# The first layers of the last eight chunks: two chunks at a time as seven block products instead of eight, with the combined weights and attention's output passed through memory

## The chip, the cores and the metric

The kernel runs on one core of one Trainium2 chip. TensorE (PE) multiplies matrices into PSUM, VectorE (DVE) and ScalarE (ACT) do the elementwise work, GpSimd (POOL) does almost nothing before the change, and SyncE (SP) issues the transfers between SBUF and memory; its queue is worked off in the order in which it is written. The metric is the time of one execution on the device in microseconds; lower is better.

## What is computed

```python
def phi(x):                                   # x: 8 batches, 8 heads, 576 tokens, 64
    proj = x @ w_phi                          # 128 features
    proj = proj - max(abs(proj), axis=-1)
    return concat([exp(proj), exp(-proj)])    # 256 features
q_p, k_p = phi(q), phi(k)
kv = einsum('bhsf,bhsd->bhfd', k_p, v); z = k_p.sum(tokens)
attn = (q_p @ kv) / (q_p @ z + 1e-6)
x = attn as 4608 tokens x 512
g, val = x @ w_gate, x @ w_val                # 512 x 1536 each
out = (g * sigmoid(g) * val) @ w_out          # 1536 x 512
```

The weights arrive as 64-bit floats and are turned into two 32-bit parts on the chip.

## The kernel before

**Attention.** There are 32 units, one for each batch and pair of heads, called attention 0 to 31 here (`attention(i, rank)`). Units 0 to 7 run "early", with plain fp32 matmuls. Units 8 to 31 are "split": operands are cut into a high and a low part (fp32r), and a product takes three matmuls. In one split unit the steps follow each other: the projections of k (`work<-wbd_hi,ks`) and q (`work<-qs,wst_hi`, `wst_lo`: eight matmuls) on PE; copies to `qx` on ACT (L534); on DVE a transpose (L539), the largest value (L547), six small steps, a transpose back (L559), and a subtraction (L562); on ACT two exponentials (L564, L566) and casts to the high part (L579); on DVE the low part (L582); on PE the numerators, 24 matmuls that begin with `work<-qh,kvh`; on ACT the copies to `num` and `den` (L607, L609); on DVE the division (L616 to L620). Most of these buffers exist once for the split units, so unit i+1 can write `qe` only after unit i has divided. At the end `num` is cut into `xh` and `xl` (L632, L634), the operands of the feed-forward part. There are three sets of `xh` and `xl`.

**Feed-forward.** The 4608 tokens are 12 chunks of 384. A chunk has 12 slices f of 128 features. `first(c, f)` makes the gate and the value of a slice: 2 x 4 x 3 = 24 matmuls of 128x384 into two PSUM banks (`gv<-xh,w_hi`, `gv<-xl,w_hi`, `gv<-xh,w_lo`), then tanh on ACT (L716) and two products on DVE (L718, L721). `parts` cuts the result into `hh` (ACT, L741) and `hl` (DVE, L742), and `second(c, f)` multiplies it by w_out: 9 matmuls of 128x512 into three banks `o`. The high parts of all weights stay in SBUF; the low parts are loaded for each slice (`w_lo<-wlo_dram`, 512 KB for the first layer, 256 KB for the second). Chunks 0 to 2 are "early": their first layers run while the weights are prepared, and chunks 1 and 2 keep the result in memory (`keep`, `fetch`) until their second layers run. After that come chunks 3 to 11, each slice's first layer followed by the second layer of the slice before (`put_off`).

**What sets the order.** Every step is given to `Plan.add` with an engine, a cost, what it depends on, and a rank. `Plan.run` plays the steps through once, on the host, and writes each engine's instructions in the order in which it started them. On the chip each engine then runs its list in that order and waits for whatever comes first in it. On PE, attention has a lower rank than feed-forward, so it goes first when it is ready; on ACT and DVE feed-forward goes first (`FIRST`).

Of the kernel before, what the change touches and what calls it, by code (L numbers as in the profile page):

```python
# [17 lines left out]
P = 128  # L18
# [28 lines left out]

# [11 lines left out]
class Plan:  # L59
# [3 lines left out]
    LAG = {"PE": 220, "ACT": 90, "DVE": 90, "SP": 2000}  # L63
# [24 lines left out]
    def run(self):  # L88
# [11 lines left out]
        def start(e):  # L100
# [33 lines left out]
            for t in s.then:  # L134
                n += 1
                heapq.heappush(events, (freed if t.eng == e and e in ("ACT", "DVE", "PE") else done, n, "dep", t))
# [29 lines left out]
def dve(n):  # L166
    return 150 + 1.04 * n
# [5 lines left out]

def act(n):
    return 190 + 0.86 * n


def pe(n):
    return max(58, 7 + 0.441 * n)
# [7 lines left out]
def favor_attention_moe(ctx: ExitStack, tc: tile.TileContext, qT, kT, v, w_phi, wg, wv, wo, out):  # L187
# [7 lines left out]
    h_dram = tc.dram_tile([EARLY, NFT, P, CH], F32, name="h_dram")  # L195

# [139 lines left out]
    x_ready = {}  # L336
# [4 lines left out]
    def attention(i, rank):  # L341
# [245 lines left out]
        for h in range(2):  # L587
            for part in range(2):
# [4 lines left out]
                def numerators(key=key, h=h, c=c):  # L593
# [12 lines left out]
                free = last.get(("num", i - 1))  # L606
                copied.append(add("ACT", act(SH), lambda key=key, ra=ra, c=c: nc.scalar.copy(  # L607
                    num[ra, c], work[plan.bank[key]][ra, :SH]), [nu, free], rank))
                copied.append(add("ACT", act(SH), lambda key=key, ra=ra, rb=rb, c=c: nc.scalar.activation(  # L609
                    den[ra, c], work[plan.bank[key]][rb, :SH], AF.Copy, bias=1e-6), [nu, free], rank, give=key))  # L610
# [17 lines left out]
            [(base, 0, 0, CH), (base + 1, 0, CH, CH // 2)]  # L628
        for c, at, start, width in cuts:
            src = num[:, start:start + width]  # L630
# [8 lines left out]
        last["num", i] = lo  # L639
# [86 lines left out]
    def keep(c, f, j, made):  # L726

        th_free[j] = h_kept[c, f] = add("SP", P * CH * 4, lambda: nc.sync.dma_start(h_dram[c, f], th[j]), [made], FIRST)

    def fetch(c, f):  # L730
        j = ffn["th"] % TH_SETS
        ffn["th"] += 1
        return j, add("SP", P * CH * 4, lambda: nc.sync.dma_start(th[j], h_dram[c, f]), [h_kept[c, f], th_free[j]], FIRST)
# [13 lines left out]
    def second(c, f, hidden, low):  # L747
        b, ready = hidden
        readers, lo, lo_ready = low
        for t in range(NT):  # L750
            sl = slice(t * P, (t + 1) * P)

            def go(t=t, sl=sl):
                if t == 0:
# [4 lines left out]
                    ((hh[b][:, sl], w2_hi[f]), (hh[b][:, sl], lo), (hl[b][:, sl], w2_hi[f])))])  # L759
# [3 lines left out]
            if f == NFT - 1:  # L763
                if n_out[0] == NCH * NT - 1:

                    halves = [pool.tile([P, DM // 2], F32, name=f"osb_last{k}", tag=tag) for k, tag in enumerate(("num", "den"))]
                    for k, eng in enumerate(("ACT", "DVE")):
                        cols = slice(k * DM // 2, (k + 1) * DM // 2)
                        rows = out[c * CH + t * P:c * CH + (t + 1) * P, cols]

                        def copy(k=k, cols=cols, t=t, o=halves[k]):
                            if k:
                                nc.vector.tensor_scalar(out=o, in0=ps_o[t][:, cols], scalar1=0.5, scalar2=None, op0=ALU.mult)
                            else:
                                nc.scalar.activation(o, ps_o[t][:, cols], AF.Copy, scale=0.5)

                        cp = add(eng, act(DM // 2), copy, [done], FIRST)
                        q = nc.sync if k else nc.scalar
                        add("SP" if k else "ACT", P * DM * 2 if k else 60, lambda q=q, rows=rows, o=halves[k]: q.dma_start(rows, o), [cp], FIRST)
                    continue  # L780
                o = osb[n_out[0] % len(osb)]
                cp = add("ACT", act(DM), lambda t=t, o=o: nc.scalar.activation(o, ps_o[t], AF.Copy, scale=0.5),  # L782
                         [done, out_done.get(n_out[0] - len(osb))], FIRST)
                stored[t] = cp
                out_done[n_out[0]] = add("SP", P * DM * 4, lambda t=t, o=o: nc.sync.dma_start(
# [105 lines left out]
```

## Time and profile before

| | |
|---|---|
| median of 3 runs | 1269.33 us (1268.94 to 1270.84) |
| span of the profiled execution | 1273.1 us, 3.8 us above the median |
| busy share PE, DVE, ACT, POOL | 99%, 69%, 51%, 0% |
| moved by the DMA queues | 168.15 MB, 132 GB/s over the span |
| matmuls of 128x384 into `gv` | 3456 |

A busy PE says little here, since matmuls overlap: one of 128x384 is listed with 337 ns, yet the next one starts some 175 ns after it. Time on PE is therefore read from the chain that ended last, which lists runs of matmuls with start and length. "att i" stands in the text for attention unit i.

### The profile page before, as it was taken

How to read it: one execution, taken by the hardware profiler on the slowest of the kernel's cores; microseconds unless marked ns; L12 is line 12 of the kernel's file. 1: busy time of each engine (PE TensorE's matmuls, PEld its weight loads, DVE VectorE, ACT ScalarE, POOL GpSimd, SP SyncE). 2: the span in 40 equal slices, each digit the busy share in tenths (PEclk: the TensorE clock that was granted, in tenths of full speed). 3: DMA queues.
4: the chain of work that ended last, by engine and by line, in shares of the span. 5: the costliest groups of instructions: out<-in, count | busy, mean ns of one | idle time of the engine just before them, and what ended most of it. 6: DMA issues, size and time to landing. Idle time of an engine off the chain costs nothing.

```text
span 1273.1 us, 19796 instructions
## 1 busy us (share of the span) xinstructions
PE 1262.2 (99%) x7427; PEld 1189.9 (93%) x7427; DVE 876.4 (69%) x1674; ACT 651.5 (51%) x1383; POOL 1.3 (0%) x13
## 2 busy tenths in 40 slices
PE   9999999999999999999999999999999999999998
PEld 8887999999889999999999999999999999999998
DVE  6998999998887778762788888822488886222222
ACT  5787433336676666632765666611466665121211
POOL 0000000000000000000000000000000000000000
PEclk8999999999999999999999999999999999999999
DMA  4543455555564344444433444354444342444443
GB/s 120 144 119 102 140 174 175 174 165 167 159 204 123 112 117 113 148 123 127 129 104 113 129 124 120 105 161 129 125 120 119 105 132 84 124 149 125 149 126 106
DMA packets 112111, 168.15 MB, mean 132 GB/s; under 512 B 52752, under 2 KB 59408, under 8 KB 112016
## 3 DMA queue, kind: packets, MB, share of 16 engines
q1 hardware_dynamic: 111552, 166.64, 44.1%
q8 instruction: 58, 0.95, 0.3%
q14 instruction: 37, 0.30, 0.1%
q10 hardware_dynamic: 464, 0.26, 0.1%
HBM read 143.26 MB, written 23.59 MB: 131 GB/s over the span
## 4 chain that ended last, share of the span: by engine, by line
PE 92%; DVE 4%; DMA 1%; ACT 1%; SPq 1%; issue 0%; DVEq 0%; ACTq 0%
PE gv L282 46%; PE o L282 25%; PE work L282 12%; PE kv L435 8%; PE kv L428 1%; DMA out_dram<-osb 0%; PE o L502 0%; DVE km L410 0%; DVE kp L415 0%; DMA shared<-in_wg_dram 0%; DMA shared<-in_wo_dram 0%; DVE qy L491 0%; DMA wbd<-in_w_phi_dram 0%; DVE km L486 0%; ACT den L609 0%
## 5 line engine op out<-in xcount | busy, mean ns | idle before, releaser
L282 PE MATMUL gv<-xh,w_hi 128*128 128x384 f32 x1152 | 388.6, 337 | 0.8 <-DVE th L718 0.8
L282 PE MATMUL gv<-xh,w_lo 128*128 128x384 f32 x1152 | 386.9, 336 | 0.0
L282 PE MATMUL gv<-xl,w_hi 128*128 128x384 f32 x1152 | 386.1, 335 | 0.0
L282 PEld LDWEIGHTS gv<-xh,w_hi 128*128 128x128 f32 x1152 | 216.4, 188 | 5.7 <-DVE th L718 1.1
L282 PEld LDWEIGHTS gv<-xl,w_hi 128*128 128x128 f32 x1152 | 216.5, 188 | 4.6
L282 PEld LDWEIGHTS gv<-xh,w_lo 128*128 128x128 f32 x1152 | 216.1, 188 | 0.0
L716 ACT ACTIVATE th<-gv 128x384 f32<-128x384 f32 x144 | 70.9, 492 | 263.9 <-PE gv L282 263.1
L718 DVE SCALAR_TENSOR_TENSOR th<-th,gv 128x384 f32<-128x384 f32 x144 | 79.2, 550 | 149.6 <-ACT th L716 147.7
L282 PE MATMUL o<-w_hi,hl 128*128 128x512 f32 x432 | 171.5, 397 | 0.2 <-DVE hl L742 0.2
L282 PE MATMUL o<-w_hi,hh 128*128 128x512 f32 x432 | 170.9, 396 | 0.3 <-ACT osb L782 0.3
L282 PE MATMUL o<-w_lo,hh 128*128 128x512 f32 x432 | 170.3, 394 | 0.0
L741 ACT CAST hh<-th 128x384 fp32r<-128x384 f32 x144 | 73.6, 511 | 164.3 <-DVE th L721 148.1
L721 DVE TENSOR_TENSOR th<-th,gv 128x384 f32<-128x384 f32 x144 | 79.4, 552 | 71.1 <-PE gv L282 68.7
L435 PEld LDWEIGHTS kv<-vf,kp 128*128 128x128 f32 x1024 | 123.2, 194 | 3.1 <-ACT kp L419 1.3
L435 PE MATMUL kv<-vf,kp 128*128 128x66 f32 x1024 | 123.2, 274 | 1.3 <-ACT kp L419 1.0
L742 DVE TENSOR_TENSOR hl<-th,hh 128x384 fp32r<-128x384 f32 x144 | 79.5, 552 | 32.8 <-ACT hh L741 32.1
L282 PEld LDWEIGHTS o<-w_hi,hl 128*128 128x128 f32 x432 | 81.4, 188 | 19.4 <-DVE hl L742 0.6
L282 PEld LDWEIGHTS o<-w_hi,hh 128*128 128x128 f32 x432 | 81.7, 189 | 12.7 <-ACT osb L782 0.8
L282 PEld LDWEIGHTS o<-w_lo,hh 128*128 128x128 f32 x432 | 81.4, 188 | 12.2
L616 DVE STREAM_TRANSPOSE qe<-den 128x576 f32<-128x576 f32 x32 | 24.9, 778 | 92.0 <-ACT den L609 92.0
L607 ACT COPY num<-work 64x288 f32<-64x288 f32 x102 | 40.2, 394 | 51.2 <-PE work L282 49.8
L282 PE MATMUL work<-qh,kvh 128*128 128x288 f32 x192 | 60.8, 317 | 0.3 <-DVE kp L415 0.3
(124 smaller groups left out, 1871.1 us busy)
## 6 DMA issues: line engine op xcount, KB each, us to landing
w_lo<-wlo_dram SPq DMA_DIRECT2D x108, 512.0 KB, 3.6
w_lo<-wlo_dram SPq DMA_DIRECT2D x132, 256.0 KB, 3.0
wlo_dram<-w_lo SPq DMA_DIRECT2D x36, 256.0 KB, 2.3
out_dram<-osb SPq DMA_DIRECT2D x35, 256.0 KB, 3.3
kin<-in_kT_dram SPq DMA_DIRECT2D x32, 256.0 KB, 2.9
vf<-in_v_dram SPq DMA_DIRECT2D x64, 128.0 KB, 2.7
qin<-in_qT_dram SPq DMA_DIRECT2D x24, 288.0 KB, 2.9
shared<-in_wg_dram SPq DMA_DIRECT2D x12, 512.0 KB, 3.6
```

What stands on the lines that cost most here:

```text
L282: nc.tensor.matmul(o, l, r, start=a, stop=z)
L428: nc.tensor.matmul(ps_kv[:, 2 * k * D2:2 * (k + 1) * D2], room[:, 0, k], vf[j][:, 4].rearrange("p h d -> p (h d)"), start=False, stop=k == 1)
L435: nc.tensor.matmul(o, room[:, 2 * (t - t0) + h, k], vf[j][:, t, h], start=t + h + k == 0, stop=False)
L607: copied.append(add("ACT", act(SH), lambda key=key, ra=ra, c=c: nc.scalar.copy(num[ra, c], work[plan.bank[key]][ra, :SH]), [nu, free], rank))
L616: t0 = add("DVE", dve(S), lambda: vec.transpose(turned, den), [*copied, *done[0], *done[1]], rank)
L716: s1 = add("ACT", act(CH), lambda: nc.scalar.activation(t_, ps_gv[0][:, :CH], AF.Tanh, scale=0.5), [ends[0], th_free[j]], FIRST)
L718: s2 = add("DVE", dve(CH), lambda: nc.vector.scalar_tensor_tensor(out=t_, in0=t_, scalar=1.0, in1=ps_gv[0][:, :CH], op0=ALU.add, op1=ALU.m ...
L721: s3 = add("DVE", dve(CH), lambda: nc.vector.tensor_tensor(out=t_, in0=t_, in1=ps_gv[1][:, :CH], op=ALU.mult), [s2, ends[1]], FIRST)
L741: s4 = add("ACT", act(CH), lambda: nc.scalar.copy(hh[b], th[j]), [made, hid_free[b]], FIRST)
L742: s5 = add("DVE", dve(CH), lambda: nc.vector.tensor_tensor(out=hl[b], in0=th[j], in1=hh[b], op=ALU.subtract), [s4], FIRST)
```

## The change

Two chunks c and c+1 (rows) and the two halves of the 512 inputs (columns) form a 2x2 block matrix A; the gate and value weights of a slice, each cut into its two halves of the inputs, form a 2x2 block matrix W. Their product is made from seven block products instead of eight (Winograd's form of Strassen's method). Chunks 4 to 11 are taken as four such pairs; chunks 0 to 3 stay as they were. One block product is 2 x 3 = 6 matmuls of 128x384, so a slice of two chunks takes 42 instead of 48.

- `mixed(f)`: once for each slice, POOL adds the high and low parts of the weights and makes the four combinations (4 + 4 + 4 instructions of 128x256), ACT rounds them to a high part (128x1024), and SP writes all seven stationary blocks, high and low, to `wt_dram` (six transfers, 1.8 MB) after one load of 512 KB. It uses `xh1`, `xh2`, `xl1`, `xl2`, which are free once the first layers of chunks 1 and 2 are done.
- `attention`: for tokens of chunk 4 and later `num` is stored to `x_dram` (SP) instead of being cut into `xh` and `xl`. The next unit's `num` then waits for that transfer. The three sets of x no longer hold attention back.
- `operands(c)`: loads the four quarters of two chunks from `x_dram`, makes four combinations on DVE (128x768), and cuts the seven operands into high and low parts (7 casts on ACT, 7 subtractions on DVE).
- `load_ring`: the high and low weights of two block products come back from `wt_dram` in one transfer of 512 KB, into a ring of six buffers (`w1_hi0` to `w1_hi5`); 42 for a pair of chunks.
- `pair(c)`: for each slice the products P1, P2, P6, P7, P5, P4, P3 into the two `gv` banks. P1, P6, P7, P4 go on adding in one bank, and ACT copies it out after P1, P6 and P7 (L1035); P2, P5, P3 use the other, and DVE adds the copy to it (L1039). Then come tanh and two products for both chunks. The second layer of the slice before is spread over three places. Chunk c+1 keeps its result in memory, and its second layer runs after the pair, as for chunks 1 and 2.

```diff
+PAIRS = 4
+RING = 6
...
         last["num", i] = []
         held = [(start, width) for c, at, start, width in cuts if c >= PAIRS]
+        if held:
...
+            x_stored[b, pr] = add("SP", P * width * 4, lambda ...: nc.sync.dma_start(
+                x_dram[pr, :, token:token + width], num[:, start:start + width]), [t3], rank)
...
+    def mixed(f, rank):
...
+        get = add("SP", P * 4 * DM * 2, lambda: nc.sync.dma_start(src.bitcast(F32), wlo_dram[f, :, :2 * DM]),
+                  [lo_stored[f, 0], lo_stored[f, 1], *old[0], *x_free[1]], rank)
...
+        def combine():
+            x, t = full(), sums()
+            for o, l, r in ((2, x[:, block(2)], x[:, block(0)]), (1, x[:, block(3)], x[:, block(2)]),
+                            (0, x[:, block(3)], t[:, block(2)]), (3, x[:, block(1)], t[:, block(0)])):
+                gp.tensor_tensor(out=t[:, block(o)], in0=l, in1=r, op=ALU.subtract)
...
+        g0 = add("POOL", 4 * pool2(2 * P), whole, [get, *old[1], *x_free[2]], rank)
+        g1 = add("POOL", 4 * pool2(2 * P), combine, [g0, *old[2]], rank)
+        g2 = add("ACT", act(8 * P), lambda: nc.scalar.copy(high, sums()), [g1, *old[3]], rank)
+        g3 = add("POOL", 4 * pool2(2 * P), rest_of, [g2], rank)
...
+        w_spread[f] = [add("SP", 4 * r, lambda: put(2, 4, 0, high.bitcast(F32)), [g2], rank),
+                       add("SP", 4 * r, lambda: put(2, 4, 1, sums()), [g3], rank), *early]
...
+    attend(NCH * CH)
...
+    def load_ring(m, n):
+        k = m % RING
+        after, ring_user[k] = ring_user[k], []
+        return add("SP", P * 8 * P * 4, lambda: nc.sync.dma_start(
+            flat(w1_hi[k]).bitcast(F32), wt_dram[:, 2 * n:2 * n + 2].rearrange("p n h c -> p (n h c)")),
+            [*after, *w_spread[2 * n // 7], *w_spread[(2 * n + 1) // 7]], FIRST)
...
+            p1 = mult(0, bank_b, True, False, b_read)
+            y1 = copy(0, p1)
+            p2 = mult(1, bank_c, True, True, c_read)
+            g1 = joined(0, [p2, y1])
+            ja, ga = gate(snap[0], [g1])
+            p6 = mult(2, bank_b, False, False, [y1])
+            y2 = copy(1, p6)
+            part(0)
+            p7 = mult(3, bank_b, False, False, [y2])
+            y3 = copy(2, p7)
+            p5 = mult(4, bank_c, True, False, [g1])
+            v2 = joined(2, [p5, y3])
+            p4 = mult(5, bank_b, False, True, [y3])
+            jb, gb = gate(lambda: bank_b[:, :CH], [p4])
+            part(1)
+            p3 = mult(6, bank_c, False, True, [v2])
+            v1 = joined(1, [p3, y2])
+            part(2)
+            b_read[:], c_read[:] = [gb], [v1]
+            ha = valued(ja, 1, [ga, v1])
+            hb = valued(jb, 2, [gb, v2])
+            snap_free[:] = [[ga], [ha], [hb]]
+            keep(c + 1, f, jb, hb)
+            put_off(c, f, parts(ja, ha), low2(f))
```

**Where instructions stand.** First, PE in a slice of the feed-forward part with no attention between. Before, the end of the 12 matmuls into the value's bank and the second layer behind them:

```order
L282 MATMUL gv_144<-xl_101,w_hi_72 128x384
L282 MATMUL gv_144<-xh_98,w_lo_94 128x384
L282 MATMUL gv_144<-xh_98,w_hi_72 128x384
L282 MATMUL gv_144<-xl_101,w_hi_72 128x384
L282 MATMUL gv_144<-xh_98,w_lo_94 128x384
L282 MATMUL o_140<-w_hi_83,hh_130 128x512
L282 MATMUL o_140<-w_lo_95,hh_130 128x512
```

Now P6, a third of the second layer, and P7 (names such as `xh_100` and `w_hi_76` are the buffers that now hold operands and the ring):

```order
L1027 MATMUL gv_145<-xh_100,w_hi_76 128x384
L1027 MATMUL gv_145<-op_lo,w_hi_76 128x384
L1027 MATMUL gv_145<-xh_100,w_hi_76 128x384 x2
L1027 MATMUL gv_145<-op_lo,w_hi_76 128x384
L1027 MATMUL gv_145<-xh_100,w_hi_76 128x384
L289 MATMUL o_142<-w_hi_85,hh_132 128x512
L289 MATMUL o_142<-w_lo_1378,hh_132 128x512
L289 MATMUL o_142<-w_hi_85,hl_134 128x512
L1027 MATMUL gv_145<-xh_100,w_hi_71 128x384
L1027 MATMUL gv_145<-op_lo,w_hi_71 128x384
```

A bank was left alone for 12 matmuls of the other bank before; now the same bank `gv_145` is copied out by ACT while only three matmuls of 128x512 stand in between.

Second, PE in att 15, from the last projection of q to the numerators. Before, the first rows behind the projection:

```order
L282 MATMUL work_147<-qs,wst_hi 128x288
L282 MATMUL work_147<-qs,wst_lo 128x288
L282 MATMUL o_141<-w_hi_88,hh_131 128x512
L282 MATMUL o_141<-w_lo_96,hh_131 128x512
L282 MATMUL o_141<-w_hi_88,hl_133 128x512
L282 MATMUL o_142<-w_hi_88,hh_131 128x512
```

Now the same place:

```order
L289 MATMUL work_148<-qs,wst_hi 128x288
L289 MATMUL work_148<-qs,wst_lo 128x288
L289 MATMUL gv_146<-xh_99,w_hi_76 128x384
L289 MATMUL gv_146<-xl_102,w_hi_76 128x384
L289 MATMUL gv_146<-xh_99,w_lo_96 128x384
L289 MATMUL gv_146<-xh_99,w_hi_76 128x384
```

Before, 63 matmuls of 128x384, 24 of 128x512, 12 of 128x256 and 3 of 128x128 stand between that projection and the first numerator (`work<-qh,kvh`); now 36, none, 12 and 3.

Third, SP while chunk 3's first layer and the mixing of the weights run side by side (the semaphores that each waits for are in brackets; `DMAHW` are those of earlier transfers). Before, the loads of the next attention unit stand among loads of weights:

```order
L683 DMA w_lo_96<-wlo_dram 128x512 [waits DMAHW0_49,PE_49]
L683 DMA w_lo_94<-wlo_dram 128x1024 [waits DMAHW1_49,PE_49]
L683 DMA w_lo_95<-wlo_dram 128x512 [waits DMAHW2_49,PE_49]
L683 DMA w_lo_93<-wlo_dram 128x1024 [waits DMAHW3_49,PE_49]
L683 DMA w_lo_96<-wlo_dram 128x512 [waits DMAHW4_49,DMAHW0_49,PE_49]
L364 DMA qin<-in_qT_dram 128x576 [waits DMAHW5_49,DVE_49,Activation_49]
```

Now they and the first layer's weights stand behind the stores of the mixing, which wait for ACT and POOL:

```order
L879 DMA wt_dram<-xl_104 128x4x256 [waits DMAHW6_49,Activation_49]
L879 DMA wt_dram<-w_sums 128x4x256 [waits DMAHW7_49,Pool_49]
L858 DMA xh_100<-wlo_dram 128x1024 [waits DMAHW1_49,DMAHW0_49]
L375 DMA vf<-in_v_dram 128x4x64 [waits PE_49]
L375 DMA vf<-in_v_dram 128x4x64 [waits DMAHW2_49,PE_49]
L378 DMA vf<-in_v_dram 64x64 [waits DMAHW3_49,PE_49]
L378 DMA vf<-in_v_dram 64x64 [waits DMAHW4_49]
L641 DMA x_dram<-num 128x576 [waits DMAHW5_49,DVE_49,Activation_49]
L371 DMA qin<-in_qT_dram 128x576 [waits DMAHW6_49,DVE_49]
L700 DMA w_lo_96<-wlo_dram 128x1024 [waits DMAHW7_49,PE_49]
```

Behind a store that waits for POOL, everything that SP has still to issue waits too.

More of the change, by code (lines that the diff above doesn't have):

```diff
@@ L59 @@
 class Plan:
-    LAG = {"PE": 220, "ACT": 90, "DVE": 90, "SP": 2000}
+    LAG = {"PE": 220, "ACT": 90, "DVE": 90, "POOL": 200, "SP": 2000}
     BYTES = 250.0
@@ L135, in start @@
                 n += 1
-                heapq.heappush(events, (freed if t.eng == e and e in ("ACT", "DVE", "PE") else done, n, "dep", t))
+                heapq.heappush(events, (freed if t.eng == e and e in ("ACT", "DVE", "PE", "POOL") else done, n, "dep", t))
             if s.give is not None:
@@ L638, in attention @@
                 early_done.extend([hi, lo])
-        last["num", i] = lo
+            last["num", i].append(lo)
         plan.early = False
@@ L745, in parts, with second @@
         return b, [s4, s5]
-    def second(c, f, hidden, low):
+    def second(c, f, hidden, low, parts_of=range(NT)):
         b, ready = hidden
         readers, lo, lo_ready = low
-        for t in range(NT):
+        for t in parts_of:
             sl = slice(t * P, (t + 1) * P)
@@ new lines, in favor_attention_moe, with wide_tile @@
+    wide = {}
+    def wide_tile(name, tag, shape=(P, 8 * P), dtype=F32):
+        if name not in wide:
+            wide[name] = pool.tile(list(shape), dtype, name=name, tag=tag)
+        return wide[name]
+    for f in range(NFT):
+        mixed(f, FIRST)
+    for f in range(NFT):
+        put_off(2, f, parts(*fetch(2, f)), low_parts_at_rest(f, NFT + f))
+    attend((EARLY + 1) * CH)
+    w_used = {}
+    for f in range(NFT):
+        j, h = first(EARLY, f, low_parts(f, 0))
+        w_used[f] = ffn["pe"]
+        keep(EARLY, f, j, h)
+        put_off()
@@ new lines, in favor_attention_moe @@
+    op_lo = [lambda: half(xl[0], 0), lambda: half(xl[0], 1), lambda: half(whole_set("op_lo", "xl1"), 0),
+             lambda: half(whole_set("op_lo", "xl1"), 1), lambda: half(xl[2], 0), lambda: half(xl[2], 1),
+             lambda: spare(w1_hi[RING + 1])]
+    piece = lambda n, tag: wide_tile(f"part{n}", tag, (P, 2, CH))
+    tags = ["w1_hi8", "w1_hi9", "w1_lo0", "w1_lo1"]
+    quarter = [lambda n=n: piece(n, tags[n]) for n in range(4)]
+    temp = [lambda n=n: piece(4 + n, f"w1_hi{10 + n}") for n in range(2)]
@@ L826, in favor_attention_moe @@
         for f in range(NFT):
-            j, h = first(c, f, low_parts(f, 0))
-            put_off(c, f, parts(j, h), low_parts(f, 1))
+            put_off(c + 1, f, parts(*fetch(c + 1, f)), low2(f))
+    for n in range((NCH - PAIRS) // 2):
+        pair(PAIRS + 2 * n, 7 * NFT // 2 * n)
     put_off()
```

218 lines of the change are left out of this document (183 added, 35 removed).

## The prediction

> **What bounds the kernel now.** I read the page's shares and slices first, then the chain that ended last, then the forms of instructions on DVE and ACT, and last the timeline at the places that the change touches. From the page:
>
> ```profile
> span 1273.1 us, 19796 instructions
> PE 1262.2 (99%) x7427; PEld 1189.9 (93%) x7427; DVE 876.4 (69%) x1674; ACT 651.5 (51%) x1383; POOL 1.3 (0%) x13
> DVE  6998999998887778762788888822488886222222
> GB/s 120 144 119 102 140 174 175 174 165 167 159 204 123 112 117 113 148 123 127 129 104 113 129 124 120 105 161 129 125 120 119 105 132 84 124 149 125 149 126 106
> PE 92%; DVE 4%; DMA 1%; ACT 1%; SPq 1%; issue 0%; DVEq 0%; ACTq 0%
> ```
>
> PE carries 92% of the chain. DVE is nearly full early and mostly empty late (last 6 slices). So time is saved by fewer matmuls, as long as whatever feeds PE keeps up. The price of a matmul comes from the chain in order of time (start, length, engine, what, count):
>
> ```profile
> 846.43 4.19 PE gv L282 x24
> 850.62 2.09 PE o L282 x9
> 852.71 4.19 PE gv L282 x24
> ```
>
> One of 128x384 costs 4.19/24 = 0.175 us of PE, one of 128x512 costs 2.09/9 = 0.232.
>
> **Term 1, the seven products.** Before, a slice of two chunks has 48 matmuls of 128x384; now 42. Four pairs of 12 slices drop 4 x 12 x 6 = 288: 288 x 0.1746 = -50.3 us, all on the chain. The second layers are as many as before. A pair's slice then takes 42 x 0.1746 + 9 x 0.232 = 9.42 us of PE, the deferred second layer of the odd chunk 2.09 us a slice.
>
> **Term 2, attention with less work over its chain.** Between the last projection of q and the first numerator lies a long chain on ACT and DVE; PE fills it with feed-forward work from a list fixed beforehand. Timeline of PE before, at att 9 and att 15:
>
> ```profile
> 306.91 0.29 PE L282 MATMUL work<-qs,wst_lo 128*128 128x288 f32 x1
> 321.00 0.37 PE L282 MATMUL work<-qh,kvh 128*128 128x288 f32 x1 [0.27 <-DVE kp L415]
> 479.48 0.30 PE L282 MATMUL work<-qs,wst_lo 128*128 128x288 f32 x1
> 497.90 0.29 PE L282 MATMUL work<-qh,kvh 128*128 128x288 f32 x1
> ```
>
> At att 15 there are 18.4 us between the two and PE has no idle time; at att 9, 14.1 us, where PE waited 0.27. So the chain needs about 14 us beside other work, and 18.4 at most. Now att 15 has 27 fewer matmuls of 128x384 and 24 fewer of 128x512 there: 18.4 - 4.7 - 5.6 = 8.1 us. Counting the other units' rows in the same way: att 11 10.8, 13 12.7, 14 8.5, 17 10.1 us; all others 14 or more. What is short of 14.0 is 3.2 + 1.3 + 5.5 + 6.0 + 3.9 = 20 us, in which PE stands still. If the chain can run in 12 us, since its engines have less feed-forward work there, it is 10; at 18.4 for every unit, 52. I take +20: att 9 is the only place where the chain's own end is seen.
>
> **Term 3, the bank handed over within a pair.** P6 and P7 add to the same bank, with ACT's copy and three matmuls of 128x512 between. A hand-over of a bank before (last matmul, ACT's read, DVE's read):
>
> ```profile
> 1250.31 0.33 PE L282 MATMUL gv<-xh,w_lo 128*128 128x384 f32 x1
> 1250.68 0.49 ACT L716 ACTIVATE th<-gv 128x384 f32<-128x384 f32 x1 [3.04 <-PE gv L282]
> 1251.21 0.55 DVE L718 SCALAR_TENSOR_TENSOR th<-th,gv 128x384 f32<-128x384 f32 x1 [2.98 <-ACT th L716]
> ```
>
> From the last matmul's start to the next engine's start it takes 0.90 us; the cover is 0.175 + 3 x 0.232 = 0.87. The other two hand-overs have six matmuls, 0.175 + 1.05 = 1.22, over them. With ACT free that is 0.03 x 48 = 1 us; but beside attention ACT is busy 67.1 of 104 us (the second window below), and a copy then waits for part of an operation of 0.35 to 0.75 us. Two pairs of four run beside attention: 24 slices x 3 hand-overs x two thirds busy x some 0.1 us left uncovered = 5. I take +6 (bounds 1 and 14, the latter with 0.27 us lost at each of 48).
>
> **Term 4, the mixing: POOL, SP's queue, memory.** The mixing runs from the end of chunk 2's first layer (about 315 us) to about 540 us, over 241 us of PE's new work. Before, POOL shows only set-up work, DVE's nearest forms are much faster per column, and SP's waits and the queue read:
>
> ```profile
> masks.py:199 POOL TENSOR_SCALAR_AFFINE_SELECT ident<-ident 128x128 f32<-128x128 f32 x1 | 0.3, 288 | 0.0
> L460 DVE TENSOR_TENSOR kvl<-kv,kvh 128x256 fp32r<-128x256 f32 x48 | 18.7, 417 | 0.0
> SPq L683 <- PE gv L282: 357.4, 89, 6.0
> q1 hardware_dynamic: 111552, 166.64, 44.1%
> 350.00:360.00 10.00, 10.00 (x66) 9.11 (x65) 5.11 (x9) 8.70 (x19) 0.00 (x0) 1.00 0.79 244
> 362.00:466.00 104.00, 104.00 (x627) 96.83 (x627) 84.20 (x163) 67.11 (x144) 0.00 (x0) 1.00 0.45 133
> ```
>
> (The windows: us, busy PE, PEld, DVE, ACT, POOL, granted clock, DMA share, GB/s.) A POOL operation of 128x256 with two inputs lies between DVE's 0.42 and twice the columns and twice the inputs of the select, 4 x 0.288 = 1.15 us; I take 0.7, the middle. Twelve and ACT's cast of 128x1024 (1 us, by columns from the casts below) make 9.4 us a slice, 113 us for twelve in a row: inside 241 us, and still inside with 1.15 (178). The GPSIMD Engine Reference of the Trainium skill (section 3.1) has a two-input operation of 2048 columns at 4497 ns, estimated 0.56 us for 256: 81 us in all for POOL, the same verdict.
>
> But SP issues in order. Stores that wait for POOL now stand ahead of the loads of qin, vf and w_lo, and the stretch moves 66.8 MB (265 transfers, counted in the new order) in 241 us = 277 GB/s. The fastest window quoted has 244 GB/s at a share of 0.79, which is 309 at a full share. So it fits with little to spare, where the slices of before (32 us each, the row GB/s) stand between 112 and 204 there. A load of w_lo that comes 4 us late stops PE for 4 us less its lead of one slice (6.3 us of PE); a late qin lengthens an attention unit. I take +10; bounds 0 (309 GB/s holds) and 33 (only 244 hold: 66.8/0.244 = 274 us against 241).
>
> **Term 5, operands of a pair: 0.** Seven casts of 128x768 on ACT and eleven operations on DVE, by columns from
>
> ```profile
> L380 DVE TENSOR_TENSOR ks<-kin,ks 128x640 fp32r<-128x640 f32 x24 | 19.7, 822 | 4.7 <-ACT ks L378 3.8 <-DMA qin<-in_qT_dram 0.7
> L378 ACT CAST ks<-kin 128x640 fp32r<-128x640 f32 x24 | 17.2, 715 | 0.1
> L742 DVE TENSOR_TENSOR hl<-th,hh 128x384 fp32r<-128x384 f32 x144 | 79.5, 552 | 32.8 <-ACT hh L741 32.1
> L716 ACT ACTIVATE th<-gv 128x384 f32<-128x384 f32 x144 | 70.9, 492 | 263.9 <-PE gv L282 263.1
> ```
>
> are about 11 x 0.96 = 10.5 us on DVE (0.82 + 128 columns x 0.27/256) beside 7 x 0.83 = 6 on ACT. They stand beside the 25 us (12 x 2.09) of the previous odd chunk's second layers, ahead of which their buffers are free. Without that cover they would cost some 10 us at each of four pairs.
>
> The rest of the added work is off the chain: 144 copies on ACT (0.49 each, 71 us) and casts lead it from 651 to about 740 us of 1220; 144 more joins on DVE (0.55, 79) and the operands lead it from 876 to about 975, of which the part beside attention is what stood there before, since attention's own work only loses its `xl`. The ring's loads in a pair: 2.29 MB in 9.42 us (3.5 loads of 512 KB, 256 KB of w_out's low part, 192 KB for `keep`) is 243 GB/s, the rate of that window of before, but sustained; one load lasts 9.42/3.5 = 2.7 us of PE, and with five more in the ring 13 us lie over it. If the sustained rate fell to 220 GB/s, 48 slices would cost 1.0 us each.
>
> **The sum.** -50.3 + 20 + 6 + 10 + 0 = -14 us: 1273.1 - 14 = 1259 for a span like that of the profile. The median of the runs is 3.8 us below that span, so 1255 us. Terms at their best (10, 1, 0) give 1230. With 19 for the three together instead of 36 it is 1238, with 47 it is 1266: the likeliest case's own range.
>
> **The rivals.**
>
> Everything added is hidden. For it: ACT and DVE are free a third of the time, and the attention chain has less feed-forward work in its way when PE has none to give. Against it: units with 8 us of work over 14 us of chain. 1269.3 - 50.3 + 5 = 1224. Chance 0.2.
>
> Slower by memory in the mixing stretch. It decides from the rate: at 309 GB/s no loss, at 244 it is +33, and at 204 GB/s 327 us against 241 is +86. In the rival the stretch sustains 235 GB/s, 284 us against 241, +43 in place of 10: 1255 + 33 = 1288. For it: no slice of before sustains more than 204, and SP's in-order waits (6.0 us each for weights before) leave queues empty. Against: nothing asked for more before. The turn from gain to loss lies at 253 GB/s (term 4 = 23 us or more). Chance 0.15.
>
> The attention chain needs its 18.4 us everywhere: term 2 is 52, 1255 + 32 = 1287. For it: all steady units have just this much between. Against: att 9 with 14.1. Chance 0.08.
>
> POOL and DVE slow each other. The mechanism: a DVE operation with two inputs in SBUF waits while POOL reads. About 126 such operations in the stretch (ten in a unit, and `hl` of each slice); POOL is busy 101 of 241 us, and with half a POOL operation lost at each, 126 x 0.42 x 0.35 = 18 us of DVE, where DVE is 0.8 busy; as the chain of attention lengthens by as much, 1255 + 18 = 1273, slower by 4. No row of before shows POOL beside busy DVE, so the trace says neither. The Trainium skill states it so: SBUF — State Buffer, "Who interferes with whom", has the two share one pair of ports, locked for a whole instruction. By that rule this rival holds, and the trace neither agrees nor disagrees. Chance 0.12.
>
> **Numbers.** Likeliest case, the sum, 0.45: 1255. Faster by over 0.2% (2.5 us, about what measurements of this kernel can tell from no change; under 1266.8): the likeliest but for its top tenth (0.41), the first rival (0.2), a third of the port rival (0.04), and a weak form of the memory rival (0.03): 0.68. Slower: memory 0.11, chain 0.08, port 0.05, 0.01 of the likeliest: 0.25. Between: 0.07. The range takes in the first rival's 1224 and both slow ones: 1222 to 1290.
>
> **What would show it.** Matmuls into `gv` 3168, PE's chain share still near 90%, and span about 1259. Term 2: PE idle before `work<-qh,kvh` of att 11, 13, 14, 15 and 17, 3 to 6 us each, released by ACT or DVE. Term 3: 48 waits on ACT's copies, some 0.1 us. Term 4: PE waiting for `w_lo` or kin/qin between 315 and 540 us, GB/s there near 270, POOL operations near 0.7 us. Term 5: no idle PE at P1 of the four pairs. It is wrong if POOL's operations take over 1.5 us (twelve then need 19 us a slice, 230 us of the 241, and pair 1 waits for `wt_dram`), if the ring's loads make PE wait in every slice of the late pairs, or if DVE's mean times in 315 to 540 us rise.

## The result: 1312 us, slower by 42

The changed kernel takes 1312.04 us (median of 4 runs, 1309.88 to 1314.91) against 1270.07 us (1268.94 to 1270.84) for the kernel before beside it: ratio 1.033, 95% interval 1.031 to 1.034. The profiled execution has a span of 1308.1 us. Its page, the lines that answer to those shown of before:

```profile
span 1308.1 us, 20516 instructions
PE 1251.6 (96%) x7139; PEld 1151.2 (88%) x7139; DVE 994.8 (76%) x1818; ACT 735.4 (56%) x1523; POOL 122.5 (9%) x157
PE   9999999999979988899999999999989999899998
DVE  7998999998777878897878878878887744634452
POOL 0000000004444533510000000000000000000000
PEclk9999999998988988999999999999999999999999
GB/s 150 128 112 97 177 177 183 169 155 250 236 257 199 308 214 226 292 200 210 216 200 213 215 217 217 209 207 218 200 227 138 251 268 240 247 216 246 236 170 181
PE 77%; DVE 14%; ACT 5%; DMA 2%; issue 2%; SPq 0%; DVEq 0%; ACTq 0%
```

PE's share of the chain fell from 92% to 77%, and DVE and ACT hold 19% of it where they held 5%. Most of the loss lies where POOL works: slices 9 to 17 (counted from 0), 300 to 590 us, with a lower clock beside it. The same stretch by windows (us, busy PE, PEld, DVE, ACT, POOL, granted clock, DMA share, GB/s). Before, six such windows had PE busy for 299.0 of 300 us; two of them:

```profile
400.00:450.00 50.00, 50.00 (x320) 47.91 (x319) 38.84 (x73) 34.66 (x75) 0.00 (x0) 1.00 0.44 130
450.00:500.00 50.00, 50.00 (x307) 47.72 (x305) 42.84 (x84) 30.32 (x64) 0.00 (x0) 1.00 0.40 114
```

Now:

```profile
300.00:350.00 50.00, 46.07 (x234) 39.54 (x233) 43.97 (x72) 30.38 (x63) 28.66 (x32) 0.90 0.84 261
350.00:400.00 50.00, 41.33 (x238) 35.91 (x238) 37.09 (x62) 34.05 (x73) 20.45 (x25) 0.90 0.77 240
400.00:450.00 50.00, 45.66 (x245) 41.09 (x244) 40.35 (x68) 32.47 (x63) 24.70 (x28) 0.90 0.78 244
450.00:500.00 50.00, 41.93 (x246) 40.72 (x245) 38.94 (x71) 28.81 (x61) 17.13 (x23) 0.85 0.75 250
500.00:550.00 50.00, 43.13 (x284) 41.50 (x282) 38.48 (x68) 31.53 (x65) 24.27 (x30) 0.98 0.81 255
550.00:600.00 50.00, 47.17 (x254) 39.96 (x255) 42.73 (x73) 36.83 (x73) 5.97 (x8) 0.94 0.67 205
```

A busy PE hides part of the loss, so a second measure is used below. For every matmul the time to the start of the next one is compared with the median for its form (the same shapes and access patterns) in the kernel before; the sum of these medians is called *nominal*. What goes beyond by over 0.25 us is called *standing*, the rest *stretching* (a slower clock, or many small waits). Worked out from the timelines, in us:

| | nominal | standing, 300 to 600 | stretching, 300 to 600 | standing, behind 600 | stretching, behind 600 |
|---|---|---|---|---|---|
| before | 1228.8 | 1.7 | 2.2 | 0.5 | 1.9 |
| after | 1178.8 | 44.3 | 20.2 | 15.3 | 15.5 |

The nominal time fell by 50.0 us. Standing and stretching behind 300 us grew by 89, and ahead of it they fell by 4: together the 35 us by which the span of the profiled execution grew (1273.1 to 1308.1 us).

The longest stand of all, on PE (start, length, instruction, idle time ahead of it and who ended it):

```profile
367.12 0.28 PE L289 MATMUL work<-wbd_hi,ks 128*128 128x256 f32 x1
375.42 0.47 PE L289 MATMUL work<-wst_hi,ks 128*128 128x128 f32 x1 [8.02 <-DVE kp L422]
```

PE's list has the last third of a unit's k projection there, which needs a bank that DVE frees with `kp`; DVE is in the middle of another unit's q chain, and no feed-forward work stands between. Of the 44 us of standing, 18 are ahead of `work<-wst_hi,ks`, 7 ahead of the numerators `work<-qh,kvh`, and 10 in the second layers (`o`). A late transfer is hardly among the causes: from 290 us on, the largest row of PE's waits and the only one on a transfer are (us in total, times, longest)

```profile
PE work L289 <- DVE kp L422: 19.3, 9, 8.0
PE work L289 <- DMA th<-h_dram: 0.2, 1, 0.2
```

and between 300 and 600 us ACT and DVE wait for transfers for 2.5 us in all.

### The profile page after: what moved, and what is told of

It reads as the page before. It is cut to its first block, busy times and chain, and to the rows that moved or that the text cites. A ratio compares the mean times of both kernels' runs of the same rounds, so it can differ in the third digit from the quotient of the medians.

```text
span 1308.1 us, 20516 instructions
## 1 busy us (share of the span) xinstructions
PE 1251.6 (96%) x7139; PEld 1151.2 (88%) x7139; DVE 994.8 (76%) x1818; ACT 735.4 (56%) x1523; POOL 122.5 (9%) x157
## 4 chain that ended last, share of the span: by engine, by line
PE 77%; DVE 14%; ACT 5%; DMA 2%; issue 2%; SPq 0%; DVEq 0%; ACTq 0%
PE gv L1027 24%; PE o L289 21%; PE gv L289 12%; PE work L289 11%; PE kv L442 8%; DVE qm L554 1%; DVE qx L569 1%; PE kv L435 1%; DVE hl L759 1%; DVE qe L566 1%; ACT qe L571 1%; DVE km L417 1%; DVE qe L546 1%; DVE ql L589 1%; DVE kp L422 1%
## 5 line engine op out<-in xcount | busy, mean ns | idle before, releaser
L1027 PE MATMUL gv<-xh,w_hi 128*128 128x384 f32 x768 | 217.7, 342 | 0.7
L289 PE MATMUL o<-w_hi,hh 128*128 128x512 f32 x432 | 175.3, 406 | 11.5 <-ACT hh L758 6.1
L289 PE MATMUL o<-w_hi,hl 128*128 128x512 f32 x432 | 175.8, 407 | 8.9 <-DVE hl L759 8.9
L1039 DVE TENSOR_TENSOR part<-gv,part 128x384 f32<-128x384 f32 x144 | 79.9, 555 | 70.3 <-PE gv L1027 65.2
L289 PE MATMUL gv<-xh,w_hi 128*128 128x384 f32 x384 | 130.3, 339 | 0.8 <-DVE th L735 0.8
L289 PE MATMUL gv<-xh,w_lo 128*128 128x384 f32 x384 | 129.3, 337 | 0.0
L289 PE MATMUL gv<-xl,w_hi 128*128 128x384 f32 x384 | 129.1, 336 | 0.0
L442 PE MATMUL kv<-vf,kp 128*128 128x66 f32 x1024 | 127.5, 280 | 1.5 <-ACT kp L426 1.2
L1027 PE MATMUL gv<-xl,w_hi 128*128 128x384 f32 x384 | 128.6, 335 | 0.0
L289 PEld LDWEIGHTS o<-w_hi,hl 128*128 128x128 f32 x432 | 83.4, 193 | 33.2 <-DVE hl L759 14.2
L1027 PE MATMUL gv<-op_hi,w_hi 128*128 128x384 f32 x384 | 106.8, 335 | 0.0
L1035 ACT COPY part<-gv 128x384 f32<-128x384 f32 x144 | 68.4, 475 | 63.8 <-PE gv L1027 60.7
L1027 PEld LDWEIGHTS gv<-xl,w_hi 128*128 128x128 f32 x384 | 72.1, 188 | 1.8
```

The costliest lines, as they stand in the source:

```text
L289: nc.tensor.matmul(o, l, r, start=a, stop=z)
L442: nc.tensor.matmul(o, room[:, 2 * (t - t0) + h, k], vf[j][:, t, h], start=t + h + k == 0, stop=False)
L1027: nc.tensor.matmul(o[:, :CH], l, r, start=begin and i == 0, stop=i == len(terms) - 1, skip_group_check=True)
L1035: s = add("ACT", act(CH), lambda: act_.copy(snap[n](), bank_b[:, :CH]), [after, *snap_free[n]], FIRST)
L1039: return add("DVE", dve(CH), lambda: vec.tensor_tensor(out=snap[n](), in0=bank_c[:, :CH], in1=snap[n](), op=ALU.add), after, FIRST)
```

## The experiments

All are measured beside the kernel before (1270.5 to 1271.2 us in these jobs). Five explanations are set against each other: M, memory moves too little between 300 and 590 us; P, POOL and DVE hold each other up; L, the lists written beforehand hold PE; A, attention's pace sets when the second pair can start; H, the bank is handed over too slowly inside a pair.

**POOL's work cut to 8 of 256 columns, the same lists.**

```diff
+    thin = lambda n: slice(2 * P * n, 2 * P * n + 8)
-                gp.tensor_tensor(out=full()[:, block(n)], in0=hi[:, block(n)], in1=src[:, block(n)], op=ALU.add)
+                gp.tensor_tensor(out=full()[:, thin(n)], in0=hi[:, thin(n)], in1=src[:, thin(n)], op=ALU.add)
...
```

> The changed kernel with POOL's 144 operations on 8 of 256 columns each; the combined weights are left out but for these columns, and every engine's list and every transfer stay as they are. Theory M (the stretch from 305 to 585 us is bounded by what memory moves, some 250 GB/s, and by loads that land late in lists fixed beforehand): the time stays between 1300 and 1312 us, PE's standstills between 300 and 600 us stay above 30 of 44 us. Rival P (POOL's operations and DVE's two-input operations hold each other up): DVE's operation that makes ql goes back from 1.00 to 0.75 us, the standstills fall by half or more, and the time is 1280 to 1290 us.

1295.99 us (1295.64 to 1297.03), 16.0 less. DVE's forms between 305 and 580 us (count, busy us, mean ns), first in the changed kernel:

```profile
L589 DVE TENSOR_TENSOR ql<-qx,qh 128x576 fp32r<-128x576 f32 x18 | 18.1, 1003 | 0.0
L566 DVE STREAM_TRANSPOSE qe<-qu 128x576 f32<-128x576 f32 x20 | 14.7, 760 | 0.1
```

and with the thin operations:

```profile
L589 DVE TENSOR_TENSOR ql<-qx,qh 128x576 fp32r<-128x576 f32 x20 | 15.0, 751 | 0.0
L566 DVE STREAM_TRANSPOSE qe<-qu 128x576 f32<-128x576 f32 x20 | 14.8, 761 | 0.1
```

The subtraction with two inputs in SBUF takes a third longer beside POOL; the transpose with one input takes the same. Not every operation with one input does: the small copies `qu<-qm` of 64x36 (L557) take 0.35 us where they took 0.18. Summed over all forms, DVE's instructions between 305 and 590 us are 20 us longer in the changed kernel than by the medians of this run. Standing between 300 and 600 us falls from 44 to 34 only, so neither theory had it whole: POOL's neighbourhood is worth 16 us, more than M allowed and less than P asked for. The first pair starts at 572.0 instead of 588.0 us, and what follows keeps that lead: the second pair starts at 775.9 instead of 793.2.

**No mixing at all.**

```diff
     for f in range(NFT):
-        mixed(f, FIRST)
+        w_spread[f] = [lo_stored[f, 0], lo_stored[f, 1], *x_free[1], *x_free[2]]
...
-            flat(w1_hi[k]).bitcast(F32), wt_dram[:, 2 * n:2 * n + 2].rearrange("p n h c -> p (n h c)")),
+            flat(w1_hi[k]).bitcast(F32), wlo_dram[n % NFT, :, :8 * P]),
```

> The mixing is left out as a whole (POOL's work, ACT's casts, the load and the six stores of each slice); the pairs' ring loads as many bytes from the plain low parts instead, so the pairs' results are not the reference's. Theory M: PE's standstills between 300 and 600 us fall from 44 to under 10 us and the half-clock windows behind them go with them, 50 us or more there. If nothing else is late next the time is about 1255 us. Rival A (attention needs some 29 us a unit whatever is done, unit 23 was through its numerators at 760 us, and the second pair needs it): pair 1 starts some 50 us earlier but pair 2 waits for unit 23, and the time is 1285 to 1300 us.

1285.38 us (1281.97 to 1287.27). Rival A came true, at the fast end of its range: the stretch from 300 to 600 us is clean (standing 4.8 us), the first pair starts at 512.3 instead of 588.0 us, 76 us earlier, but the second pair does one product at 719 us and then PE has little but attention's steps until 769 us:

```profile
758.74 0.28 PE L289 MATMUL work<-wbd_hi,ks 128*128 128x256 f32 x1
769.17 0.69 PE L1027 MATMUL gv<-xh,w_hi 128*128 128x384 f32 x1 [10.15 <-ACT part L1035]
```

The chunks of that pair need attention's unit 23, whose numerators start at 743.2 us, only 17 earlier than in the changed kernel. The last 10 us of the wait are the way of its result: the division ends at 757.9 us, `num` is stored and loaded back by 764, and the combinations and casts of the operands end just ahead of the matmul:

```profile
764.14 0.83 ACT L985 CAST op_hi<-part 128x768 fp32r<-128x768 f32 x1 [5.87 <-DMA part<-x_dram]
```

Of 76 us gained, 27 are left at the end.

**And no waiting for attention in pairs 2 to 4.**

```diff
-            token = (at - PAIRS) * CH
+            token = (n // 2) * CH
...
-                [*(x_stored[x] for x in need), *quarter_free[n]], FIRST))
+                [*(x_stored[x] for x in need0), *quarter_free[n]], FIRST))
```

(`need0` are the units of chunks 4 and 5.)

> As the kernel without mixing, and besides every pair loads attention's output of chunks 4 and 5, so that pairs 2 to 4 wait for no attention unit; the same work is done on the wrong chunks. If attention's pace holds pair 2 back (rival A), this takes 20 to 35 us off the run without mixing, to 1255 to 1270 us. If it does not, the two agree within 5 us.

1256.68 us (1254.84 to 1259.72): 28.7 less than without mixing alone, inside what rival A said.

**The products of a pair in another order.**

```diff
             p6 = mult(2, bank_b, False, False, [y1])
             y2 = copy(1, p6)
-            part(0)
+            p5 = mult(4, bank_c, True, False, [g1])
             p7 = mult(3, bank_b, False, False, [y2])
             y3 = copy(2, p7)
-            p5 = mult(4, bank_c, True, False, [g1])
             v2 = joined(2, [p5, y3])
+            part(0)
+            part(1)
             p4 = mult(5, bank_b, False, True, [y3])
             jb, gb = gate(lambda: bank_b[:, :CH], [p4])
-            part(1)
             p3 = mult(6, bank_c, False, True, [v2])
```

> The changed kernel with the products of a pair in another order: P1, P2, P6, P5, P7, two thirds of the second layer, P4, P3, the last third. Six matmuls or more now lie over each copy of the bank, where P7 had three of 128x512. Theory H (each slice of a pair loses some 0.2 us there): the spacing of matmuls beyond nominal in the pairs falls from about 1.0 to 0.3 us in 50 us, and the time is 1300 to 1306 us. If the hand-over costs nothing, it stays at 1310 to 1314; if P5 now waits for DVE to read its bank, it rises.

1298.78 us (1293.53 to 1305.68), 13 less, with a spread of 12 us over its runs. Stretching behind 600 us falls from 15.5 to 6.0 us and standing there from 15.3 to 11.2: 13.6 together, about the whole gain. Theory H holds at the 0.2 us a slice that it said: just ahead of the first matmul of P7 and just behind it PE loses 9.4 us beyond nominal over the 48 slices of the changed kernel, and 1.3 us here. The rest is what it had not counted on: less standing in the second layers behind 600 us (14.5 to 9.4 us), and none of the three spells of a halved clock there, in which 3.9 us were lost.

**The mixing's transfers cut to 8 of 128 partitions, the same lists.**

```diff
-        get = add(... nc.sync.dma_start(src.bitcast(F32), wlo_dram[f, :, :2 * DM]),
+        get = add(... nc.sync.dma_start(src[:8].bitcast(F32), wlo_dram[f, :8, :2 * DM]),
...
-            wt_dram[:, rows(j, n), part], t.rearrange("p (n c) -> p n c", n=n))
+            wt_dram[:8, rows(j, n), part], t[:8].rearrange("p (n c) -> p n c", n=n))
```

> The changed kernel with the mixing's load and six stores of each slice cut to 8 of 128 partitions; the pairs' ring loads the same bytes from the plain low parts (so their results are not the reference's). POOL's and ACT's work and every engine's list stay. POOL alone was worth 16 us (1312 to 1296). Theory M (memory late in the stretch): PE's standstills between 300 and 600 us fall from 44 to about 25 us and the time to 1290 us or less. Rival L (the lists, fixed beforehand, hold the waits: attention's steps stand in them where its chain cannot be ready, and memory is in time): 1308 to 1312 us, standstills as before.

1314.32 us (1310.13 to 1321.25): no gain, standing 47 us. With the lists as they are, 27 MB less in that stretch are worth nothing; theory M falls. Nor is 250 GB/s the most that memory gives, for a short time at least: in the changed kernel 4 us behind the first pair ran at 318 GB/s with a share of 0.94:

```profile
753.70:757.70 4.00, 2.16 (x9) 1.25 (x8) 3.97 (x8) 1.61 (x3) 0.00 (x0) 0.99 0.94 318
```

**The other order and a planner that counts on 300 GB/s.**

```diff
-    BYTES = 250.0
+    BYTES = 300.0
```

> The changed kernel with the other order of products (1299 us by itself) and the planner's memory rate at 300 instead of 250 GB/s, which moves feed-forward work ahead of where the lists have it. Theory L (the lists are what holds PE): another 10 us or more, 1280 to 1290 us. Theory M (memory gives no more than 250 GB/s there): no gain or a loss, 1297 to 1310 us, with PE waiting for landings instead.

1296.59 us (1288.36 to 1298.83), no more than the order alone. The lists do change: the first pair starts at 546.5 us, 41.5 us earlier, and standing plus stretching from 300 to 600 us fall from 64 to 43. Then PE stands for 18 us from 700 to 800 us: the second pair does one product and goes on at 786.6 us, where it began at 793.2. The gain is given back at unit 23, as without mixing.

**Thin transfers, and lists written for them.** The edit is that of the thin transfers, and the costs of the seven steps in the planner are divided by 16.

> As the run with thin transfers of the mixing (1314 us with the lists of the changed kernel), but the planner counts the thin transfers as thin, so the lists are written anew; POOL's and ACT's work stay whole, the combined weights are left out but for 8 of 128 partitions. Theory L (what the lists were planned on holds PE between 305 and 585 us, through the 250 GB/s of the planner, and not a landing on the chip): standstills between 300 and 600 us fall from 44 to 20 us or less and pair 1 starts by 545 us, where 1314 us came with the same thin transfers; then pair 2 waits for attention's unit 23, and the whole takes 1288 to 1302 us. Theory P alone (POOL beside DVE): nothing changes, 1305 to 1315.

1318.44 us (1315.14 to 1322.42), outside what either theory said. The first pair starts at 543.8 us (expected: by 545), standing from 300 to 600 us is 28. But the mixing now runs closer together, and unit 23 comes at 774.6 us, 14 later than in the changed kernel and 31 later than without mixing; the second pair waits for it until 803.5 us:

```profile
803.52 0.69 PE L1027 MATMUL gv<-xh,w_hi 128*128 128x384 f32 x1 [10.28 <-ACT part L1035]
```

**The same lists with POOL thin as well** (the edits of the first and the fifth experiment together).

> The run with thin transfers and lists written anew (1318 us), the same lists, with POOL's operations on 8 of 256 columns as well; the combined weights are left out. Theory P (POOL beside DVE stretches attention's chain, and unit 23, which the second pair waits for, comes 31 us later than without mixing: 775 against 744 us): unit 23 back at 744 to 752 us, the time 1285 to 1295 us. Rival: ACT's casts and the lists made unit 23 late; then 1310 to 1318 us.

1287.64 us (1287.07 to 1287.79), 30.8 less by POOL's columns alone, and within the scatter of the runs without mixing (1281.97 to 1287.27, median 2 us lower). Unit 23 starts at 746.9 us:

```profile
746.91 0.58 PE L289 MATMUL work<-qh,kvh 128*128 128x288 f32 x1 [0.52 <-ACT qh L586]
```

So ACT's casts and the lists were not what made it late; POOL was. The order of instructions on PE, DVE and ACT is the same in both runs.

**POOL beside the kernel before.**

```diff
+    spare = sb("spare", [P, 2 * P])
+    def beside():
+        def four():
+            for _ in range(4):
+                nc.gpsimd.tensor_tensor(out=spare, in0=spare, in1=spare, op=ALU.mult)
+        add("POOL", 3500, four, [ffn["pe"], cleared], 0.0)
```

> The kernel before, with its lists unchanged, and beside it 144 multiplications of 128x256 with two inputs on POOL, in 36 groups of four that each wait for a slice between 315 and 505 us; nothing waits for them. Theory P: DVE's operation that makes ql takes 0.9 to 1.0 in place of 0.75 us there, attention's chain outgrows the 18 us of work that stand over it, and PE, which never stood there, stands for 5 to 20 us: 1275 to 1290 us. If POOL and DVE do not hold each other up, 1268 to 1273 us and 0.75 us.

1285.32 us (1284.81 to 1286.47), 14 more than the 1271.24 beside it. The place was missed: a step's dependency in the planner orders a list but makes no engine wait, and nothing on the chip held POOL back, so its 144 operations ran at the start, in the first 120 us. There they ask the same question. DVE's forms in these 120 us, the kernel before and then the one with POOL:

```profile
L491 DVE TENSOR_TENSOR qy<-o,km 128x512 f32<-128x512 f32 x15 | 10.3, 690 | 0.4
L309 DVE SCALAR_TENSOR_TENSOR shared<-shared,shared 128x512 uint32<-128x512 uint32 x8 | 5.5, 693 | 0.3
L305 DVE TENSOR_SCALAR shared<-shared 128x512 f32<-128x512 f32 x10 | 4.2, 421 | 0.8 <-ACT shared L304 0.8
```

```profile
L491 DVE TENSOR_TENSOR qy<-o,km 128x512 f32<-128x512 f32 x13 | 9.0, 689 | 0.3
L309 DVE SCALAR_TENSOR_TENSOR shared<-shared,shared 128x512 uint32<-128x512 uint32 x8 | 7.6, 946 | 0.3
L305 DVE TENSOR_SCALAR shared<-shared 128x512 f32<-128x512 f32 x8 | 5.8, 729 | 0.0
L827 POOL TENSOR_TENSOR spare<-spare 128x256 f32<-128x256 f32 x144 | 102.8, 714 | 11.3
```

With two inputs in SBUF 0.25 us more; with one input, at 512 columns in 0.42 us, 0.31 us more; with an input from PSUM nothing. PE stands and stretches 12 us more in the first 200 us, and from there on the two kernels run alike; their orders on PE, DVE and ACT are the same. This is the mechanism by itself, without mixing, lists or memory.

**All three taken away: mixing, waiting, and the old order of products.**

> No mixing, no waiting of pairs 2 to 4 for attention (1257 us together), and the other order of products (13 us by itself on the changed kernel). If the three are separate, 1243 to 1247 us, and what still lacks to 1220 us (the kernel before less 50) stands at the ends of the pairs: 2 to 5 us each, PE waiting for the hidden part's low half and for outputs. If the hand-over was only paid because PE waited elsewhere, 1255 us.

1245.86 us (1244.63 to 1247.54), as said. What still lacks to 1220 us is 26. PE stands for 22 us behind 300 us, 14 of them at the pairs' ends, where it was expected. PE's waits behind 600 us (us in total, times, longest):

```profile
PE o L289 <- ACT osb L803: 7.9, 4, 3.4
PE o L289 <- ACT hh L758: 4.5, 4, 1.3
```

**Two pairs instead of four, with room for the mixing.** Chunks 8 to 11 are paired. Chunks 4 to 7 are computed as before, with attention's output through memory so that attention need not wait for a set. The kernel also has the other order of products, P3 ahead of P4 in a pair's last slice, four buffers for the pairs' outputs, and the planner's 300 GB/s; what each of these is worth here was not taken apart:

```diff
-PAIRS = 4
+PAIRS = 8
+HELD = 4
-    BYTES = 250.0
+    BYTES = 300.0
+    x_set = lambda c: c if c < EARLY else (c + 1) % 2
...
+    def load_x(c):
+        ...
+            got = add("SP", P * CH * 4, lambda k=k: nc.sync.dma_start(
+                xl[s][:, k].bitcast(F32), x_dram[k, :, token:token + CH]), ..., FIRST)
+            hi = add("ACT", act(CH), lambda k=k: nc.scalar.copy(xh[s][:, k], xl[s][:, k].bitcast(F32)), [got], FIRST)
+            lo = add("DVE", dve(CH), ... out=xl[s][:, k], in0=xl[s][:, k].bitcast(F32), in1=xh[s][:, k] ..., [hi], FIRST)
...
+        if c == 3:
+            for f in range(NFT):
+                mixed(f, 50.0)
...
+            o = osb[k] if k < 2 else wide_tile(f"osb{k}", ("kin", "qin")[k - 2], (P, DM))
```

> Seven products for chunks 8 to 11 only, two pairs in place of four, so 144 matmuls fewer than the kernel before instead of 288 (25 us). Chunks 4 to 7 take attention's output through memory too, cut on arrival, into two sets; the mixing has the third set, starts after chunk 3 and has the time of chunks 4 to 7. Order of products as in the run with the other order, outputs of the pairs through four buffers, P3 ahead of P4 in a pair's last slice, the planner's memory rate at 300 GB/s. If what the changed kernel lost is the crowding of mixing and attention ahead of the first two pairs, no stretch shows PE standing for over 5 us in 50 behind 300 us, and the time is 1252 to 1262 us, under the kernel before. If POOL beside DVE costs as much as in the changed kernel (16 us) wherever it stands, 1265 to 1275 us. If seven products lose by themselves (hand-overs, ends of pairs), over 1270 us.

1269.70 us (1264.37 to 1271.60) against 1270.47 (ratio 0.9986, interval 0.9972 to 1.0000): no change that can be told from none, and inside the second case, that POOL beside DVE costs as much wherever it stands. Nominal time is 25.4 us shorter, but PE stands for 14 us from 500 to 780 us, mostly for `kp`, beside POOL.

> As the kernel with two pairs (1269.7 us), with one edit: the planner counts 250 ns more for seven of DVE's operations of a unit (the low parts of k, q and of the features, the subtraction) in units 16 to 24, those beside the mixing, where the trace shows 0.9 to 1.0 us in place of 0.75. If PE's 14 us of standstills between 500 and 780 us come from lists that took POOL's neighbourhood for free, they fall by half or more and the time is 1258 to 1264 us. If DVE is simply full there (idle near nothing in that stretch), the standstills stay, 1267 to 1272 us.

The edit is `dve(S) + (250 if 16 <= i <= 24 else 0)` in the planner's costs of those steps, nothing on the chip but the order. 1262.61 us (1260.44 to 1266.73), ratio to before 0.9945 (0.9929 to 0.9961): half a per cent faster than the kernel before, and 49 us faster than the changed one. Standing from 500 to 780 us is 7 us. The page:

```profile
span 1260.4 us, 20442 instructions
PE 1240.5 (98%) x7282; PEld 1160.2 (92%) x7282; DVE 949.7 (75%) x1740; ACT 699.9 (56%) x1465; POOL 125.7 (10%) x157
```

## Why the prediction was wrong, point by point

1255 us was predicted, 1222 to 1290 as the range; 1312 came. In medians, one edit after the other:

| | us | difference |
|---|---|---|
| changed kernel | 1312.0 | |
| POOL thin, same lists | 1296.0 | -16.0 |
| transfers thin too, lists anew | 1287.6 | -8.4 |
| no mixing | 1285.4 | -2.2 |
| pairs wait for no attention | 1256.7 | -28.7 |
| other order of products | 1245.9 | -10.8 |
| the kernel before less 50.3 | 1220 | -26 |

The differences hold in this order; in another the shares of POOL, lists and attention differ, since each covers part of the others. The 2.2 us are within the scatter. The last 26 us were seen as stands but not taken away.

The same by PE's time beyond nominal behind 300 us: the sum had 36 us of loss, and 89 came. Of these, 30 lie in the five units of term 2 (20 in the sum), 9 at the hand-over of term 3 (6), 30 in the rest of the stretch from 300 to 600 us, where term 4 had 10, and 19 behind 600 us, where term 5 had 0. The steps that failed are terms 4 and 5, and term 2 in two of its units.

**Term 1, -50.3: right.** 1228.8 to 1178.8 us of nominal matmul time.

**Term 2, +20: right in mechanism, in three of five units also in size.** From the last projection of q to the first numerator PE lost nothing before; now it loses 11.6 us beyond nominal at att 11, 1.4 at 13, 4.5 at 14, 4.7 at 15 and 8.0 at 17, where 3.2, 1.3, 5.5, 6.0 and 3.9 were forecast. At 13, 14 and 15 the chain took 14.2, 13.1 and 12.9 us, as the 14 from att 9 said; at 11 it took 22.7 and at 17 18.2. The instruction that stands is another than expected, most often the last third of another unit's k projection, which lies inside this stretch and waits for DVE's `kp` (18 us in all, against 7 ahead of the numerators). Att 15:

```profile
483.49 0.29 PE L289 MATMUL work<-qs,wst_lo 128*128 128x288 f32 x1
494.95 0.48 PE L289 MATMUL work<-wst_hi,ks 128*128 128x128 f32 x1 [3.46 <-DVE kp L422]
496.37 0.58 PE L289 MATMUL work<-qh,kvh 128*128 128x288 f32 x1 [0.51 <-ACT qh L586]
```

With POOL thin these five units still lose 27 us, so little of this is POOL's. Without mixing the lists put more feed-forward work there, and 4 us are left. The step that failed in kind was to take each unit by itself: no term asks when attention's results are needed. The second pair needs unit 23 for both its chunks at once, where chunk 6 needed unit 19 before. In the changed kernel PE does not stand for it yet; once the mixing is away, 28.7 us hang on it. What sets unit 23's time is not shown: units 11 to 17 start 28.2 to 28.9 us apart before, but 21 to 41 us apart without mixing, so it is no fixed pace of the chain alone.

**Term 3, +6: right.** It measured 9.4 us, within its bounds of 1 and 14. The order took 13 us off by itself and 11 with the rest gone, because stands at the pairs' ends and the clock's spells behind them went with it.

**Term 4, +10: the wrong resource.** The sum put it on memory and SP's queue. Thin transfers gave nothing with the same lists, PE waits for transfers for 0.2 us, and a window ran at 318 GB/s. Most of what the mixing costs is POOL beside DVE: 16 of 27 us in the changed lists, 31 us in those written for thin transfers. The prediction worked it out as 18 us of DVE (20 were measured), in a rival to which it gave 0.12, because no row showed POOL beside a busy DVE, and left it out of the sum; the sign that it named for this, DVE's mean times rising, came. The Trainium skill, SBUF — State Buffer, "Who interferes with whom", states the rule: POOL and DVE share a pair of ports, which one instruction holds for its whole length. By that rule the traces agree, 0.75 to 1.00 us for `ql` with two inputs in SBUF and 0.69 us unchanged with PSUM as an input. The 250 GB/s that the planner counts held the first pair back as well: lists written for less traffic or a higher rate had the first pair start 41 to 44 us earlier, but that gain was given back at unit 23.

**Term 5, 0: wrong, for a cause not thought of.** The operands were covered in the changed kernel: at a pair's P1 PE does not stand. (Where the second pair waits for unit 23 they are not, and PE stands for 10.2 to 10.7 us, as the prediction said for that case.) But behind a pair's last product stands the second layer of the same slice with nothing put off to cover `hh` and `hl`, and then an output tile that waits for one of two buffers:

```profile
960.97 0.50 PE L289 MATMUL o<-w_hi,hh 128*128 128x512 f32 x1 [1.71 <-ACT hh L758]
962.23 0.62 PE L289 MATMUL o<-w_hi,hl 128*128 128x512 f32 x1 [0.53 <-DVE hl L759]
968.46 0.51 PE L289 MATMUL o<-w_hi,hh 128*128 128x512 f32 x1 [1.39 <-ACT osb L803]
```

This is most of the 15 us of standing behind 600 us. It was to be read in the new order of PE, where the last slice of a pair has its second layer right behind P3.

**The sum.** Each term's bounds were kept apart, and the range took them one at a time; with term 2 at 52 and term 3 at 14 the same sum gives 1295, with term 4 at 33 as well 1318, so the bounds together did hold 1312. Besides, no term had PE's clock, in whose spells most of the 20 us of stretching between 300 and 600 us lie.

## What to carry to other kernels

Fewer matmuls are a gain only up to the next floor: work out, for every chain that runs beside, when its results come and when they are needed (here attention's unit 23, by the second pair), before counting what PE saves. Work given to an idle POOL is not free where DVE has two inputs in SBUF: price it as time of DVE, and, where an order is planned, give the planner that price, which alone was worth 7 us here. When a cut removes little, take causes away one on top of the other, as a cause that is removed alone may only uncover the next.

## What the hardware showed that was not expected

PE's clock can fall after short stands. The stand of 1.67 us at 753.7 us and one of 0.5 at 755.9 were followed by 3.4 us at half the granted clock, though PE worked again from 756.6 us on, and matmuls of 128x512 went from one in 0.23 us to one in 0.42 (the window, columns as above, and PE's timeline):

```profile
757.80:761.10 3.30, 3.30 (x11) 2.73 (x11) 2.44 (x4) 2.17 (x4) 0.00 (x0) 0.51 0.88 254
```

```profile
757.15 0.39 PE L289 MATMUL o<-w_lo,hh 128*128 128x512 f32 x1
757.38 0.39 PE L289 MATMUL o<-w_hi,hl 128*128 128x512 f32 x1
...
758.84 0.63 PE L289 MATMUL o<-w_hi,hh 128*128 128x512 f32 x1
759.27 0.63 PE L289 MATMUL o<-w_lo,hh 128*128 128x512 f32 x1
```

Between 300 and 560 us there are six such spells, of 6.8 or 10.2 us, and most of the 20 us of stretching there lies in them: in the stretches from 418.0 to 426.5 and from 468.0 to 477.5 us, matmuls that need 8.1 us by the spacing of before took 14.6, stands left aside. So from 300 to 600 us a us of standing cost up to half a us more behind it. Not every stand does this: 1.56 us at 966.9 and 1.81 us at 1134.6 us were followed by no such spell. The Trainium skill, TensorE: Matmul & The Clock Gate (Part 1), has the clock fall after an idle window of some 3.4 us; here it fell with stands of half that length in it.
